# Sliding-window attention and an ELU feed-forward on one core: constants by VectorE arithmetic, the first batch in two halves, x in block order in a ring

## The chip, the cores and the metric

The kernel runs on one core of one Trainium2 chip. The metric is device time in microseconds, the median of several runs, lower is better. A core has five engines that run their own instruction streams and meet at semaphores: TensorE (PE), VectorE (DVE), ScalarE (ACT), GpSimd (POOL) and SyncE (SP), beside 16 DMA engines that the queues of SP and GpSimd feed. PE reads SBUF and writes PSUM, which has eight banks of 128 x 512 float32.

## What is computed

Attention over 8 batches, 8 heads, 576 positions, head size 64, causal with a window of 128 and a slope per head (ALiBi); its output is laid out as 4608 tokens of 512 features and goes through a two-layer feed-forward with ELU.

```python
scores = scale * np.matmul(q, k.transpose(0, 1, 3, 2))
bias = slopes[:, None, None] * (-np.abs(rel))[None, :, :]
mask = (rel >= 0) & (rel < 128)
scores = np.where(mask, scores + bias[None], -1e9)
attn = softmax(scores)
x = np.matmul(attn, v).transpose(0, 2, 1, 3).reshape(B * S, H * D)
h = x @ w_in                                   # 512 -> 2048
g = np.where(h > 0, h, np.exp(np.minimum(h, 0)) - 1)
out = g @ w_out                                # 2048 -> 512, float32
```

## The kernel before

All products are in float16 with float32 sums. Positions 0 to 511 of a batch are four blocks of 128, positions 512 to 575 are its **tail**. Inside a block the 128 positions stand in the order (j, i) for position 4i + j, which comes from the loads: four neighbouring positions lie in one partition row (`stq`, L76), and PE's transposes (L209) take them apart. Queries, keys and the columns of E are all in this **block order**; v is loaded so that its rows agree (L96, four loads of 32 partitions per block of 128).

*Attention* goes by units (a batch and a pair of heads, 32 units). Of a unit:

- `transposes` (L209, 8 on PE) and two copies from PSUM into QK (L215, DVE). QK holds 64 rows of the head and 64 rows of bias: a row of positions, a row of ones, and rows that push block pairs outside the window to a large negative score. These rows are the same for all batches and are filled once.
- `scores` (L245, PE), in two halves of 512 columns for each head (half 0: key blocks 0 and 1, half 1: 2, 3 and the tail), each followed by an exponential on ACT into E (L249).
- `cut` (L253, DVE): the minimum of E (1024 columns) and a table, `band`, that is 60000 inside the window and 0 outside it.
- `values` (L262) and `values_tail` (L273, L274) on PE. VP holds v in 64 columns and ones in the next 64, so the product has the sums of E beside the numerators, in the other 64 partitions.
- `log_den` (L280) and `inv_den` (L284) on ACT: 1/den as exp(-ln den).
- `normalize` (L288, DVE): numerator times 1/den into xT, the transposed x, once per head. Here the block order is undone: the access patterns of all three operands walk (n, j, i), and the output is written to (n, i, j), so that columns of xT are tokens in order. For a batch's tails `normalize_tail` (L306) needs no reordering.

*Feed-forward* goes by blocks of 512 tokens (9) and chunks of 128 of the 2048 (16): 144 steps of `hidden` (L316, four PE products over the 512 features, 512 tokens wide, into a PSUM bank `hp` of which there are two; exponential on ACT, L319; clip on POOL, L320) and `elu` (L325, DVE, reads `hp` and so frees the bank). `output` (L337) multiplies 128 tokens by w_out, 16 products into one bank; ACT copies it to `ob` (L341), and one DMA from SP stores 128 rows (L343).

*The order* is written out by hand, in **slots**. A unit begins every 4 slots (`APS`) and its steps lie at fixed slots behind that. Slot s also has hidden step m = s - LAG, the ELU of step m - 1, and the output products of step m - 16. LAG is 16 + 5 = 21, one batch of attention. In the text of a slot hidden comes first, then ELU, then the attention steps, then output. Each engine executes its own instructions in exactly this order.

*Ahead of slot 0* all constants are built (L118 to L193): the identity, `band` and the window rows by GpSimd's affine_select, then (since TQ and TK must be complete) the bias rows of all 8 heads by DVE (L186) and ACT (L190), and the ones and zeros of VP by DVE (L192, L193). Between them stand in GpSimd's queue the casts of v (L105) and the loads of the weights (L381, L384).

Of the kernel before, what the change touches and what calls it, by code (L numbers as in the profile page):

```python
# [19 lines left out]
def kernel(  # L20
# [15 lines left out]
    NTB = NTOK // 512  # L36
    APS = 4
    ABS = NP * APS
    LAG = ABS + 5
    MID = S // 2  # L40

# [20 lines left out]
    w_in_sb = [const.tile([128, FF], F16, name=f"wi{c}", tag=f"wi{c}") for c in range(4)]  # L62
    w_out_sb = const.tile([128, NFC, DM], F16, name="wo")
    xT = const.tile([128, 4, NTOK], F16, name="xT")


    stq, stt = {}, {}

    def load_qk(b, hs=None):
# [4 lines left out]
        h0, h1 = hs or (0, H)  # L74
        return [
            (lambda w=w, src=src: nc.gpsimd.dma_start(  # L76
                stq[b][:, w, h0:h1, :, :].rearrange("p h j d -> p h (j d)"),
                src[b, h0:h1, 0:512, :].rearrange("h (p j) d -> p h (j d)", j=4)))
            for w, src in ((1, k), (0, q))
        ]  # L80

    def load_tail(b):
        return [
            (lambda w=w, src=src: nc.gpsimd.dma_start(
                stt[b][:, w, :, :], src[b, :, 512:576, :].rearrange("h s d -> s h d")))
            for w, src in ((1, k), (0, q))
        ]

    vf = {}

    def load_v(b, n):

        vf[b, n] = stage.tile([128, H, D], F32, name="vf", tag="vf", bufs=3)
        if n < 4:
            for j in range(4):
                nc.sync.dma_start(  # L96
                    vf[b, n][32 * j:32 * j + 32, :, :],
                    v[b, :, 128 * n + j:128 * n + 128:4, :].rearrange("h p d -> p h d"))
        else:
            nc.sync.dma_start(vf[b, n][0:64, :, :],  # L100
                              v[b, :, 512:576, :].rearrange("h p d -> p h d"))
# [6 lines left out]

    nc.scalar.preload_act_table_set("natural_log_exp_and_others")

    with tc.manual_schedule():
        for hp in range(NP):
            for f in load_qk(0, (2 * hp, 2 * hp + 2)):
                f()
        for f in load_tail(0):
            f()

        make_identity(nc, ident)  # L118

        nc.vector.memset(band, BIG)  # L120

        def keep(cols, pattern, base, cm):
            for h in range(4):
                r = slice(32 * h, 32 * h + 32)
                o = band[r, cols]
                if len(pattern) > 1:
                    o = o.rearrange("p (n j i) -> p n j i", j=4, i=32)
                nc.gpsimd.affine_select(out=o, in_=o, compare_op=ALU.is_ge, fill=0.0,  # L128
                                        base=base(h), pattern=pattern, channel_multiplier=cm)

        W2 = [[128, 2], [1, 4], [4, 32]]
        W1 = [[128, 1], [1, 4], [4, 32]]
        neg = lambda p: [[-x, n] for x, n in p]
# [3 lines left out]
        keep(slice(768, 896), W1, lambda h: -h, -4)  # L137
        keep(slice(896, 960), [[-1, 64]], lambda h: 127 - 128 + h, 4)
        keep(slice(960, 1024), [[1, 64]], lambda h: -32 * h, -1)
# [54 lines left out]
        for n in range(3):  # L194
            load_v(0, n)
        for n in range(5):
            cast_v(0, n)
            if n < 2:
                load_v(0, n + 3)
# [255 lines left out]
```

## Time and profile before

| | us |
|---|---|
| median of 3 runs (433.31 to 434.66) | 434.52 |
| the profiled execution, its own time | 432.81 |
| its span, first to last instruction | 431.1 |
| first scores on PE | 43.72 |
| first hidden product | 79.5 |
| first output product | 127.6 |
| PE / DVE / ACT / POOL busy | 343.0 / 287.7 / 241.8 / 169.8 |

A row of a group reads: line, engine, operation, output<-inputs, shapes, count | busy us, mean ns of one | idle time of the engine ahead of them, and what ended it. A row of the timeline reads: start us, duration us, engine, line, operation. PE's products are pipelined, so the time from one start to the next says more than a product's own duration. PEclk is the share of its full clock that PE was granted.

### The profile page before, as it was taken

What the parts mean: (1) busy time and instruction counts of PE and PEld (TensorE: products, weight loads), DVE (VectorE), ACT (ScalarE), POOL (GpSimd) and SP (SyncE); (2) the same over time, 40 slices, a digit from 0 to 9 for tenths busy, and PEclk for the clock granted to TensorE, in tenths of its full rate; (3) what the DMA queues carried; (4) which work ended last, traced back from release to release, by engine and by line L of the source; (5) the groups of instructions that cost most, each with busy time, mean ns of one, the idle gap of its engine ahead of it and who ended that gap; (6) DMA issues with size and microseconds to landing.
All of it is one profiled execution on the core that took longest, in us unless ns stands there. A gap on an engine that the chain in (4) does not pass through costs nothing.

```text
span 431.1 us, 6246 instructions
## 1 busy us (share of the span) xinstructions
PE 343.0 (80%) x2240; PEld 187.6 (44%) x2240; DVE 287.7 (67%) x396; ACT 241.8 (56%) x445; POOL 169.8 (39%) x289
## 2 busy tenths in 40 slices
PE   0100556766699989998998999899989989999985
PEld 0100434443355545554554555455545544444432
DVE  1018666789878888988898787889888763334400
ACT  1005556566777676676667777766767754434411
POOL 8887323146245423633452355233322223333300
PEclk9999955699999999999999999999999999999999
DMA  9406999929214733661293238230000001101011
GB/s 139 44 1 123 202 191 193 121 53 129 42 24 82 116 82 77 90 120 50 62 133 76 75 61 126 78 90 29 26 24 26 26 24 49 40 36 49 26 56 66
DMA packets 72127, 32.91 MB, mean 76 GB/s; under 512 B 48544, under 2 KB 66976, under 8 KB 72096
## 3 DMA queue, kind: packets, MB, share of 16 engines
q0 software_dynamic: 27872, 13.63, 24.9%
q1 hardware_dynamic: 44224, 18.89, 17.0%
q8 instruction: 17, 0.28, 0.3%
q14 instruction: 14, 0.11, 0.1%
HBM read 36.70 MB, written 9.44 MB: 107 GB/s over the span
## 4 chain that ended last, share of the span: by engine, by line
PE 49%; DVE 30%; POOL 8%; DMA 5%; issue 4%; ACT 3%; POOLq 0%; ACTq 0%; DVEq 0%
PE hp L316 20%; PE op L337 18%; DVE xT L288 13%; DVE g L325 7%; DVE QK L215 7%; DMA stt<-in_q_dram 4%; PE av L262 4%; POOL band L128 3%; PE sp L245 3%; PE tp L209 2%; POOL stq L76 2%; DVE xT L306 1%; DVE E L253 1%; DMA vf<-in_v_dram 1%; ACT e L319 1%
## 5 line engine op out<-in xcount | busy, mean ns | idle before, releaser
L320 POOL TENSOR_SCALAR e<-e 128x512 f32<-128x512 f32 x144 | 90.0, 625 | 216.8 <-ACT e L319 209.1
L316 PE MATMUL hp<-xT,wi 128*128 128x512 f16 x576 | 149.5, 382 | 23.7 <-DVE g L325 23.6
L319 ACT ACTIVATE e<-hp 128x512 f32<-128x512 f32 x144 | 86.0, 597 | 111.6 <-PE hp L316 109.0
L337 PE MATMUL op<-wo,g 128*128 128x512 f16 x576 | 145.9, 379 | 2.9 <-ACT ob L341 2.9
L325 DVE SCALAR_TENSOR_TENSOR g<-e,hp 128x512 f16<-128x512 f32 x144 | 97.1, 687 | 67.9 <-POOL e L320 66.0
L316 PEld LDWEIGHTS <-wi 128*128 128x128 f16 x576 | 56.1, 98 | 93.4 <-issue 32.3
L288 DVE TENSOR_TENSOR xT<-av,rden 64x512 f16<-64x512 f32 x64 | 83.5, 1304 | 2.0
L249 ACT ACTIVATE E<-sp 128x512 f16<-128x512 f32 x128 | 72.5, 595 | 7.1 <-PE sp L245 6.3
L337 PEld LDWEIGHTS <-g 128*128 128x128 f16 x576 | 52.2, 98 | 50.4 <-issue 4.0
L245 PE MATMUL sp<-QK 128*128 128x256 f16 (+2 forms) x384 | 47.4, 249 | 30.6 <-issue 27.4
L245 PEld LDWEIGHTS <-QK 128*128 128x128 f16 x384 | 34.5, 103 | 47.5 <-issue 32.3
L215 DVE COPY QK<-tp 64x1024 f16<-64x1024 f16 x64 | 44.0, 688 | 15.0 <-PE tp L209 14.4
L253 DVE TENSOR_TENSOR E<-E,band 128x1024 f16<-128x1024 f16 x64 | 44.0, 688 | 7.6 <-ACT E L249 7.6
L280 ACT ACTIVATE lden<-av 64x512 f32<-64x512 f32 x64 | 37.5, 587 | 14.7 <-PE av L262 13.9
L262 PE MATMUL av<-E,VP 128*128 128x256 f16 (+1 forms) x256 | 37.6, 272 | 9.2 <-DVE xT L288 8.2
L262 PEld LDWEIGHTS <-VP 128*128 128x128 f16 x256 | 25.5, 102 | 26.1 <-issue 12.0
L341 ACT COPY ob<-op 128x512 f32<-128x512 f32 x36 | 21.5, 597 | 17.9 <-PE op L337 17.9
L105 POOL TENSOR_SCALAR VP<-vf 128x512 f16<-128x512 f32 (+1 forms) x40 | 26.2, 656 | 11.3 <-DMA vf<-in_v_dram 10.5
L209 PE MATMUL tp<-ident,stq 128*128 128x128 f16 x256 | 22.1, 236 | 0.3 <-ACT E L249 0.3
L190 ACT ACTIVATE QK<-TK 64x576 f16<-64x576 f16 (+1 forms) x8 | 3.2, 451 | 32.3 <-DVE QK L180 32.3
L284 ACT ACTIVATE rden<-lden 128x512 f32<-128x512 f32 x32 | 20.2, 630 | 1.0
L176 DVE MEMSET TQ<- 1x576 f16 x1 | 0.5, 538 | 26.3 <-POOL TQ L173 26.3
(44 smaller groups left out, 147.3 us busy)
## 6 DMA issues: line engine op xcount, KB each, us to landing
out_dram<-ob SPq DMA_DIRECT2D x36, 256.0 KB, 2.0
vf<-in_v_dram SPq DMA_DIRECT2D x128, 64.0 KB, 2.4
stq<-in_k_dram POOLq DMA_DIRECT2D x7, 512.0 KB, 6.0
stq<-in_q_dram POOLq DMA_DIRECT2D x7, 512.0 KB, 7.4
wi<-in_moe_w_in_dram POOLq DMA_DIRECT2D x4, 512.0 KB, 9.4
wo<-in_moe_w_out_dram POOLq DMA_DIRECT2D x4, 512.0 KB, 20.1
vf<-in_v_dram SPq DMA_DIRECT2D x8, 128.0 KB, 3.0
stq<-in_k_dram POOLq DMA_DIRECT2D x4, 128.0 KB, 5.9
```

The lines of the kernel that those rows point to most:

```text
L215: nc.vector.tensor_copy(QK[0:64, 2 * hp:2 * hp + 2, :, 0:512].rearrange("p h w (n a i) -> p (h w) n a i", a=2, i=32)[:, :, :, odd, :], t[r ...
L245: nc.tensor.matmul(s[:, o:o + n], kq[:, 1, kc:kc + 128], kq[:, 0, qc:qc + n], start=True, stop=True)
L249: nc.scalar.activation(ex[b, hp, g][:, 512 * half:512 * half + 512], s, AF.Exp, scale=0.125)
L253: nc.vector.tensor_tensor(out=e, in0=e, in1=band, op=ALU.min)
L262: nc.tensor.matmul(a[:, o0:o0 + w], vp[:, n, hp, lo:lo + 128], e[:, e0:e0 + w], start=st, stop=sp)
L280: nc.scalar.activation(lden[b, hp][r, :], avt[b, hp, g][r, :], AF.Ln)
L288: nc.vector.tensor_tensor(out=xT[r, hp, b * S:b * S + 512].rearrange("p (n i j) -> p n j i", j=4, i=32), in0=avt.pop((b, hp, g))[r, :].rea ...
L316: nc.tensor.matmul(p, w_in_sb[c][:, fc * 128:(fc + 1) * 128], xT[:, c, t * 512:(t + 1) * 512], start=(c == 0), stop=(c == 3))
L319: nc.scalar.activation(e, p, AF.Exp)
L320: nc.gpsimd.tensor_scalar(out=e, in0=e, scalar1=1.0, scalar2=0.0, op0=ALU.min, op1=ALU.max)
L325: nc.vector.scalar_tensor_tensor(out=gs[t][:, fc, :], in0=es.pop((t, fc)), scalar=1.0, in1=hps.pop((t, fc)), op0=ALU.subtract, op1=ALU.max)
L337: nc.tensor.matmul(ops[t], gs[t][:, fc, ts * 128:(ts + 1) * 128], w_out_sb[:, fc, :], start=(fc == 0), stop=(fc == NFC - 1))
```

## The change

*Constants.* GpSimd makes four iotas (row number, column number, positions), and VectorE makes everything from them by arithmetic: the identity as column == row, `band` as (distance from the middle)^2 <= 4060, the window rows by a bitwise and of position minus 8 x row. `band`'s first 512 columns come ahead of slot 0, the rest in slot 7. Bias rows are filled head by head in the slots (`bias_rows`: ACT copies the query side, DVE the key side). The ones of VP are now GpSimd's.

*Order at the start.* The first batch's attention runs in two passes: for each pair of heads, every two slots, the first half of the scores, a cut of 512 columns, `values_half` for tokens 0 to 255, `den_half`, `norm_half`; from slot 8 on, every four slots, the same for the second half and the tail. The first half's scores borrow the two `hp` banks. E has 9 buffers, since a pair's E lives until its second half. LAG is 13. Weights are loaded by chunks in the slots (`load_wi` takes 512 columns of all 512 rows), from slot 0 on; v of batch 0 is loaded behind a memset on GpSimd that holds it back behind the loads of q and k.

*Blocks.* The first 512 tokens are two blocks of 256, then 512 as before: 160 hidden steps, of which 32 are of half width, and 189 slots instead of 181.

*x.* xT has 1728 columns (three batches) and is used as a ring; a block that crosses its end is computed in two pieces (8 products instead of 4). Its columns stay in block order, so `normalize` writes one piece of 512. The rows of the output are then in block order too, and each tile is stored by several DMAs of 32 rows, every fourth row of the output, or of 64 rows for a tail.

```diff
-    LAG = ABS + 5
+    RING = 3 * S
...
-    xT = const.tile([128, 4, NTOK], F16, name="xT")
+    xT = const.tile([128, 4, RING], F16, name="xT")
...
-        make_identity(nc, ident)
-        nc.vector.memset(band, BIG)
-        for c0 in (0, 256, 512):
-            keep(slice(c0, c0 + 256), W2, lambda h: -h, -4)
-            keep(slice(c0, c0 + 256), neg(W2), lambda h: 127 + h, 4)
...
+        V.tensor_scalar(out=ident, in0=col, scalar1=rowf, scalar2=None, op0=ALU.is_equal)
...
+        V.tensor_scalar(out=bt[:, 0:256], in0=posi[:, 0:256], scalar1=kmid, scalar2=None,
+                        op0=ALU.subtract)
+        V.tensor_tensor(out=bt[:, 0:256], in0=bt[:, 0:256], in1=bt[:, 0:256], op=ALU.mult)
+        V.tensor_scalar(out=band[:, 0:256], in0=bt[:, 0:256], scalar1=4060.0, scalar2=BIG,
+                        op0=ALU.is_le, op1=ALU.mult)
+        V.tensor_copy(band[:, 256:512], band[:, 0:256])
...
+        def bias_rows(h):
+            c = 8.0 * 2.0 ** (-8.0 * (h + 1) / H)
+            nc.scalar.copy(QK[64:128, h, 0, :], TQ[64:128, :])
+            V.tensor_copy(QK[g_, h, 1, :], TK[g_, :])
+            V.tensor_scalar(out=QK[r_, h, 1, :], in0=TK[r_, :], scalar1=c, scalar2=None, op0=ALU.mult)
...
+        FIRST = ((0, 0, 0, 256), (1, 128, 256, 128))
+        SECOND = ((2, 256, 512, 256), (1, 256, 384, 128), (3, 384, 768, 128))
...
         def normalize(b, hp, g):
-            nc.vector.tensor_tensor(
-                out=xT[r, hp, b * S:b * S + 512].rearrange("p (n i j) -> p n j i", j=4, i=32),
-                in0=avt.pop((b, hp, g))[r, :].rearrange("p (n j i) -> p n j i", j=4, i=32),
-                in1=rden[b, hp][o, :].rearrange("p (n j i) -> p n j i", j=4, i=32), op=ALU.mult)
+            c = xcol(b * S)
+            V.tensor_tensor(out=xT[NUM[g], hp, c:c + 512], in0=avt.pop((b, hp, g))[NUM[g], :],
+                            in1=rden[b, hp][DEN[g], :], op=ALU.mult)
...
+        blocks = [(0, 256), (256, 256)] + [(512 * i, 512) for i in range(1, NTOK // 512)]
...
+            cuts = [(0, n)] if a + n <= RING else [(0, RING - a), (RING - a, n)]
+            for u0, u1 in cuts:
+                x0 = xcol(c0 + u0)
+                for c in range(4):
+                    nc.tensor.matmul(p[:, u0:u1], w_in_sb[:, c, fc * 128:(fc + 1) * 128],
+                                     xT[:, c, x0:x0 + u1 - u0], start=(c == 0), stop=(c == 3))
...
-                nc.sync.dma_start(out[r0:r0 + 128, :], ob)
+                    for p0, rows in rows_of(c0 + 128 * ts):
+                        nc.sync.dma_start(rows, ob[p0:p0 + rows.shape[0], :])
...
+        F = 8
+        base = lambda b: F if b == 0 else F + 16 * b
+        LAG = F + 5
```

How the change stands in the instruction streams, at three places. GpSimd (POOL) behind the first loads of q and k; in the program of before:

```order
L84 DMA stt<-in_q_dram 64x8x64
masks.py:197 MEMSET ident 128x128
masks.py:199 ISA
masks.py:199 AFFINE_SELECT ident<-ident 128x128
L128 AFFINE_SELECT band<-band 32x256 x24
L128 AFFINE_SELECT band<-band 32x128 x4
L128 AFFINE_SELECT band<-band 32x64 x8
L141 IOTA posi 128x512
L143 IOTA posi 128x64
L165 MEMSET TK 32x2x128
```

and in the changed one, where the iotas stand behind the first two of the eight loads:

```order
L72 DMA stq<-in_k_dram 128x2x256
L72 DMA stq<-in_q_dram 128x2x256
L119 ISA
L119 IOTA row 128x1
L120 IOTA col 128x128
L121 IOTA posi 128x512
L123 IOTA posi 128x256
```

The selections and GpSimd's part of TQ and TK (14 more rows in before) are gone. VectorE (DVE) ahead of the first copy of transposed heads (tp into QK); before, the rows of TQ and TK, eight heads' bias rows (only the first are shown), VP:

```order
L176 MEMSET TQ 1x576
L177 TENSOR_SCALAR TQ<-posi 1x576
L176 MEMSET TK 1x576
L177 TENSOR_SCALAR TK<-posi 1x576
L180 MEMSET QK 128x8x128
L186 TENSOR_SCALAR QK<-TK 64x576
L186 TENSOR_SCALAR QK<-TK 64x64
L186 TENSOR_SCALAR QK<-TQ 64x576
```

and now, the end of the arithmetic (gi and gt are the window and position rows on their way to TQ and TK) and the first copies:

```order
L169 TENSOR_SCALAR gi<-posi,gof 32x768
L170 TENSOR_SCALAR gi<-gi 32x768
L171 TENSOR_SCALAR TQ<-gi 32x768
L173 TENSOR_SCALAR TK<-gi 32x768
L175 TENSOR_SCALAR is_159<-rowf 128x1
L176 TENSOR_SCALAR is_160<-rowf 128x1
L177 TENSOR_SCALAR isx<-is_160 128x1
L178 TENSOR_SCALAR gt<-posi 32x768
L179 TENSOR_SCALAR TK<-gt,is_159,is_160 32x768
L181 TENSOR_SCALAR TQ<-gt,isx,is_159 32x768
```

VectorE now waits for GpSimd's iotas alone, and two heads' bias rows follow its copies instead of eight ahead of them. SP's queue, where the first outputs are stored between loads of v:

```order
L100 DMA vf<-in_v_dram 64x8x64
L343 DMA out_dram<-ob 128x512 x2
L96 DMA vf<-in_v_dram 32x8x64 x8
L343 DMA out_dram<-ob 128x512
L96 DMA vf<-in_v_dram 32x8x64 x8
```

```order
L89 DMA vf<-in_v_dram 32x8x64 x8
L405 DMA out_dram<-ob 64x512
L405 DMA out_dram<-ob 32x512 x2
L93 DMA vf<-in_v_dram 64x8x64
L405 DMA out_dram<-ob 32x512 x8
```

Each stored tile is now three or four transfers, in the same places between the loads of v.

More of the change, by code (lines that the diff above doesn't have):

```diff
@@ L111 @@
     with tc.manual_schedule():
[L112 to L116, printed above, removed]
-        make_identity(nc, ident)
-        nc.vector.memset(band, BIG)
[L122 to L129, printed above, removed]
@@ L191 @@
-        for g in range(2):
-            nc.vector.memset(VP[g][:, 4, :, :], 0.0)
-            nc.vector.memset(VP[g][:, :, :, 64:128], 1.0)
[L194 to L199, printed above, removed]
-        spt, tpt, ex, avt, tailt, lden, rden = {}, {}, {}, {}, {}, {}, {}
+        row = const.tile([128, 1], I32, name="row")
+        col = const.tile([128, 128], I32, name="col")
+        posi = const.tile([128, 768], I32, name="posi")
```

440 lines of the change are left out of this document (258 added, 182 removed).

## Prediction

> **What bounds the kernel now.** I read the page first, then busy time by stage, the start of the timeline, one unit of the middle, and the waits of the middle. The stretches below are cut at the first scores (43.7), the first hidden product (79.5), the first output product (127.6), the end of attention (343) and the last hidden product (410.6). Columns: span, then busy us of PE, PEld, DVE, ACT, POOL, the granted clock, DMA share, GB/s.
>
> ```profile
> span 431.1 us, 6246 instructions
> 43.70:79.50 35.80, 21.23 (x167) 15.79 (x168) 25.45 (x32) 20.66 (x37) 9.82 (x14) 0.69 1.28 194
> 79.50:127.60 48.10, 36.28 (x262) 21.05 (x260) 40.41 (x54) 30.86 (x57) 19.35 (x29) 0.95 0.48 68
> 127.60:343.00 215.40, 204.07 (x1429) 113.75 (x1427) 178.12 (x236) 149.58 (x278) 80.41 (x128) 1.00 0.38 72
> 343.00:410.60 67.60, 65.38 (x308) 29.62 (x307) 30.14 (x44) 31.25 (x54) 23.26 (x38) 1.00 0.10 36
> ```
>
> So there are five programs in one. Until 43.7 nothing useful runs. Then 35.8 us of attention alone, in which no engine is over 71% busy. Then 16 slots (21 to 36) of attention and hidden products in 48.1 us, 3.0 us a slot, with DVE the busiest. Then PE at 95%. Then pure products at 1.73 us a slot (67.6 us for 39 slots).
>
> The first 43.7 us, in order of time (start, duration, engine, line):
>
> ```profile
> 1.33 0.89 POOL L76 DMA_DIRECT2D stq<-in_k_dram  x1 [0.81 <-POOLq L439]
> 9.18 15.76 POOL L128 TENSOR_SCALAR_AFFINE_SELECT band<-band 32x256 f16<-32x256 f16 x36
> 15.29 1.03 PE L209 MATMUL tp<-ident,stq 128*128 128x128 f16 x8
> 31.34 0.46 DVE L177 TENSOR_SCALAR TQ<-posi 1x576 f16<-1x576 int32 x1 [1.75 <-POOL TQ L173]
> 38.38 1.12 DVE L193 MEMSET VP<- 128x1280 f16 x1 [0.33 <-DVE VP L192]
> 43.72 1.01 PE L245 MATMUL sp<-QK 128*128 128x256 f16 x6 [27.40 <-issue]
> ```
>
> The heads' data are there at 15.3, since PE transposes them, and the scores wait another 28 us for tables: GpSimd's selections until 31, then VectorE's copies into QK and the memsets of VP.
>
> The middle, one unit of four slots, PE's starts and the normalisations on DVE:
>
> ```profile
> 181.39 0.38 PE L245 MATMUL sp<-QK 128*128 128x256 f16 x2
> 182.00 2.65 DVE L288 TENSOR_TENSOR xT<-av,rden 64x512 f16<-64x512 f32 x2
> 183.36 0.54 PE L262 MATMUL av<-E,VP 128*128 128x256 f16 x4
> 183.74 0.39 PE L245 MATMUL sp<-QK 128*128 128x256 f16 x4
> 183.96 1.03 PE L337 MATMUL op<-wo,g 128*128 128x512 f16 x4
> 185.42 1.02 PE L316 MATMUL hp<-xT,wi 128*128 128x512 f16 x4 [0.43 <-DVE g L325]
> 188.45 0.55 PE L262 MATMUL av<-E,VP 128*128 128x256 f16 x4
> 189.40 1.03 PE L337 MATMUL op<-wo,g 128*128 128x512 f16 x4
> 190.26 1.03 PE L316 MATMUL hp<-xT,wi 128*128 128x512 f16 x4
> 191.12 0.38 PE L245 MATMUL sp<-QK 128*128 128x256 f16 x2
> PE hp L316 <- DVE g L325: 22.0, 25, 2.2
> ```
>
> From one start to the next a group of four 512-wide products takes 0.86 us (189.40 to 190.26), the values 0.38, a half of the scores 0.22, and the values with tails and transposes 0.95. A unit is then 8 x 0.865 + 4 x 0.22 + 0.38 + 0.95 = 9.13 us, 2.28 a slot; it took 9.73 (181.39 to 191.12), and units with a batch's tail more. The batch that starts at 182.00 repeats at 221.81, 39.8 us or 2.49 a slot. The difference is the last row: hidden products wait 22 us (from 80 to 345) for ELU, which stands on VectorE behind two normalisations of 1.3 us each.
>
> ```profile
> 221.81 1.30 DVE xT L288
> L325 DVE SCALAR_TENSOR_TENSOR g<-e,hp 128x512 f16<-128x512 f32 x144 | 97.1, 687 | 67.9 <-POOL e L320 66.0
> L288 DVE TENSOR_TENSOR xT<-av,rden 64x512 f16<-64x512 f32 x64 | 83.5, 1304 | 2.0
> L306 DVE TENSOR_TENSOR xT<-avtail,rdent 64x256 f16<-64x256 f32 x16 | 6.8, 422 | 0.2
> L253 DVE TENSOR_TENSOR E<-E,band 128x1024 f16<-128x1024 f16 x64 | 44.0, 688 | 7.6 <-ACT E L249 7.6
> L215 DVE COPY QK<-tp 64x1024 f16<-64x1024 f16 x64 | 44.0, 688 | 15.0 <-PE tp L209 14.4
> L249 ACT ACTIVATE E<-sp 128x512 f16<-128x512 f32 x128 | 72.5, 595 | 7.1 <-PE sp L245 6.3
> L280 ACT ACTIVATE lden<-av 64x512 f32<-64x512 f32 x64 | 37.5, 587 | 14.7 <-PE av L262 13.9
> L284 ACT ACTIVATE rden<-lden 128x512 f32<-128x512 f32 x32 | 20.2, 630 | 1.0
> L319 ACT ACTIVATE e<-hp 128x512 f32<-128x512 f32 x144 | 86.0, 597 | 111.6 <-PE hp L316 109.0
> ```
>
> (The first row is from the chain of waits, the others are groups: line, engine, tile, shape and count, busy us and mean ns.) VectorE's unit is 4 x 0.687 (ELU) + 2 x 0.688 (cuts) + 2 x 0.688 (copies) + 2 x 1.304 + four tail steps of 0.42 a batch = 8.5 us, 2.13 a slot.
>
> **The change, part by part.** The sum is made in slots of the new program: scores of the first pair at slot 0, first hidden product at slot 13, two half blocks until slot 44, last hidden product at slot 172, last output at 188.
>
> *Constants.* GpSimd's selections go. It issues two loads (0.89 us the first), then four iotas (0.61 the largest before), so VectorE starts at about 3.2. Its chain: 13 of the 26 steps need the one before, at 0.33 us each (L193 behind L192) 4.3; seven 768-wide ones at 0.56 (L177's 0.46 for 576, scaled) 3.9; four 256-wide ones 1.1; the small ones and the memsets 1.9. That is 11.2, done at 14.4. Bounds: 12 if dependent steps cost half of that, 17 if the 768-wide ones run like L325 and L306, where 256 more elements cost 0.265 us (0.95 each). The transposes (15.3 before) are ready by then. Adding the copies of the first transposes (1.4) and two heads' bias rows (four at 0.33), scores start at 17 instead of 43.7.
>
> *First batch in halves.* VectorE's work for a pair of heads: copies 1.38, bias rows 1.3, two half cuts and two half normalisations at 0.42 (L306's 256-wide price; a 512-wide f16 cut has half the elements of the 0.69 one), 4.4. In its order a pair's normalisations stand right behind its cuts, so it waits for values, two logarithms and one exponential of half width: about 0.6 + 2 x 0.35 + 0.4, with hand-overs 2.2. Four pairs at 6.6, tail copies 0.8, the rest of the band 1.5: from 14.4 to 43, and the first cut of the second halves with its values stands ahead of the first hidden product on PE: 44, where before had 79.5. Bounds: 36 if the waits overlap, 53 at the 35.8 us of before. The weight loads run beside it.
>
> *Slots 13 to 44.* Half blocks halve hidden, exponential, clip, ELU. Slots 13 to 28: VectorE 16 x 0.42 for ELU, 4.9 for the second halves of three pairs, 5.9 for tails, copies and cuts of the next batch, and four waits of 1.2 ahead of normalisations: 22.4 us, 1.4 a slot. Slots 29 to 44 add half outputs: per slot ScalarE (4 x 0.595 + 2 x 0.587 + 0.63)/4 + 0.35 + 0.08 = 1.48, about 1.55 with the tails, VectorE 0.42 + (7.3 - 2.75)/4 = 1.56 (7.3 is worked out in the next part), PE 1.43. The middle of before was 0.21 above its busiest engine (2.49 against 2.28), so 1.8: 28.8 us. Slots 45 to 60, full hidden and half output: PE, ScalarE and VectorE all at 1.8 to 1.84, taken as 2.15: 34.4.
>
> ```profile
> out_dram<-ob SPq DMA_DIRECT2D x36, 256.0 KB, 2.0
> vf<-in_v_dram SPq DMA_DIRECT2D x128, 64.0 KB, 2.4
> 188.99 3.88 SPq L96 DMA_DIRECT2D vf<-in_v_dram  x8
> 427.93 0.33 SPq L343 DMA_DIRECT2D out_dram<-ob  x1
> ```
>
> *x in block order.* The normalisation writes and reads in one piece; the nearest rows are L306 (422 ns for 256 elements) and L325 (687 for 512), so 0.69 instead of 1.30. Per unit VectorE falls from 8.5 to 7.3 us, 1.82 a slot, and ELU is early by 1.2 us where PE waits 0.43. PE's 2.28 is next: I take 2.33 for slots 61 to 134, 172.4 us; bounds 2.29 and 2.49. Two of eight blocks wrap around the ring: twice as many, shorter products, 1.5 us in all (0 to 4).
>
> *Stores.* Each 128-row tile leaves in three or four pieces. 0.33 us of issue each on SP, which has room (17 stores of 0.33 and 17 loads of 0.49 a batch, 14 us of 37), and two more ahead of the end: +0.7. A piece costs what v's 64 KB pieces cost, 2.4 us, not four times a whole tile's 2.0. Against this part speaks the Trainium skill, "DMA: Bandwidth & Descriptors", Rules for kernel authors: transfers to separate parts of the partitions run one after the other, so one over all 128 is better. By that rule the last tile would end about 4 us later; the issues of v, eight in 3.88 us, do not agree.
>
> *The sum.* 44 + 22.4 + 28.8 + 34.4 + 172.4 + 1.5 = 303.5. Slots 135 to 172 at 1.73: 65.7. The last outputs and store as before (410.6 to 431.1) 20.5 + 0.7. Span 390.4; the profiled execution took 432.81, 1.7 more than its span: 392.1. The median of the runs, 434.52, is 0.4% above that execution, so 393.7, **394 us**. Its own range, from the bounds, is 380 to 408.
>
> **The rivals.**
>
> *The middle does not gain* (0.12): the normalisation stays at 1.3 us since two float sources and not the order set it, or another wait takes its place. For it: nothing shows a contiguous 512-wide one. Against: L306. 74 x 0.16 more, about 406.
>
> *Latency, not work, sets the half blocks* (0.14): three small steps and four hand-overs a slot keep 2.4 us as full slots have. 16 x 1.0 + 16 x 0.6 = 25.6 more: 419. For it the 3.0 us a slot at 79.5 to 127.6, where no engine was above 84%; against, that late v loads and VectorE explain most of that.
>
> *The clock stays low* (0.09):
>
> ```profile
> 56.00:60.00 4.00, 2.17 (x18) 1.55 (x16) 2.87 (x4) 1.98 (x4) 1.12 (x2) 0.50 1.60 186
> 79.50 1.72 PE hp L316 x4
> 100.00:120.00 20.00, 13.22 (x112) 8.18 (x110) 16.94 (x24) 13.93 (x28) 8.87 (x14) 1.00 0.61 79
> ```
>
> At half clock four products take 1.72 instead of 0.86. If slots 13 to 44 ran so, PE would need 1.85 and 2.85 a slot: 7 and 17 us more, 418. The trace had full clock at 66% busy PE and half at 54%; half blocks on a full clock give about 75%. The Trainium skill, "TensorE: Matmul & The Clock Gate", Why this matters for your kernels, has PE gaps of over about 3 us drop the clock. By that rule my half blocks, whose longest wait is 2.2 us, keep it and 394 stands; if the gaps grow past it, 418.
>
> *SP becomes the bound, slower than before* (0.03): 17 stores and 17 v loads a batch on one queue, where v was loaded in the first stretch at
>
> ```profile
> 58.91 31.23 SPq L96 DMA_DIRECT2D vf<-in_v_dram  x15
> ```
>
> 2.1 us each. If transfers issue so slowly, v comes late, its cast on GpSimd waits, and each clip behind it. Slots 13 to 134 are 7.6 batches and 259 us in my sum; SP sets the pace above 259/(7.6 x 34) = 1.00 us a transfer, and from 1.16 (300 us) the kernel is slower than before. At 1.2 us: 310, so 446. Against: those fifteen waited for buffers, and eight unhindered ones took 3.88.
>
> *Loads in the way at the start* (0.07): the weights, now asked for from about 11 us on, share the engines with q, k and v; first hidden at 54 instead of 44: 404.
>
> **How the numbers follow.** The forecast has 0.55, the rivals the rest. From 380 to 418 all but the slow rival, half of the two near 418 and the forecast's lower end are held, about 0.8. A measurement tells 0.3% from no change. Only the SP rival is not faster: faster 0.96, same 0.01, slower 0.03.
>
> **What would show it.** Scores of the first pair at 17 (13 to 22), first hidden product at 44; the 64x512 normalisation near 690 ns; PE's waits for ELU in the middle under 5 us and batches 37 to 38 us apart; 1.4 and 1.8 us a slot in the half blocks at full clock; SP never waited for. A batch at 39 or more, or a first hidden product after 55, proves a step wrong.

## The result and the profile after

The changed kernel takes 395.56 us (median of 4 runs, 395.1 to 397.05), the kernel before 433.91 beside it (431.45 to 434.66): a ratio of 0.9131, 95% interval 0.9085 to 0.9177. The forecast was 394. The profiled execution took 397.05 us with a span of 395.3.

One number of the kernel before, in the table and in the prediction, is wrong. The first output product is not at 127.6 but at 120.12, as the timeline of before has it (start us, duration us, engine, line, operation):

```profile
118.31 1.03 PE L316 MATMUL hp<-xT,wi 128*128 128x512 f16 x4
...
120.12 1.03 PE L337 MATMUL op<-wo,g 128*128 128x512 f16 x4
```

The hidden products of slots 21 to 36 therefore ran from 79.3 to 118.3, 2.44 us a slot and not 3.0. No term of the sum used the 3.0, but it was the reason given for the rival in which latency sets the half blocks, and that reason was too strong.

Busy time by stage of the kernel after, cut at the first scores, first hidden product, first output, first full blocks of hidden and of output, end of attention, and the point from which output products stand alone (374.0; it answers to 410.6 in before, and the last hidden product is 2.6 us ahead of it in both; columns: span, then busy us of PE, PEld, DVE, ACT, POOL, granted clock, DMA share, GB/s):

```profile
16.39:45.08 28.69, 13.08 (x87) 8.33 (x88) 19.91 (x46) 15.53 (x30) 11.55 (x16) 1.00 1.16 174
45.08:73.70 28.62, 20.47 (x183) 15.95 (x182) 19.01 (x41) 18.54 (x45) 14.27 (x26) 0.88 0.94 142
73.70:100.40 26.70, 23.67 (x217) 16.76 (x214) 23.25 (x42) 21.30 (x47) 12.84 (x24) 1.00 0.61 90
100.40:134.00 33.60, 31.36 (x235) 18.09 (x233) 28.15 (x44) 26.40 (x51) 15.74 (x26) 1.00 0.57 87
134.00:312.00 178.00, 177.52 (x1370) 109.01 (x1368) 133.86 (x206) 131.87 (x244) 68.53 (x110) 1.00 0.41 74
312.00:374.00 62.00, 60.34 (x291) 27.70 (x290) 26.07 (x40) 27.29 (x48) 21.49 (x35) 1.00 0.15 36
374.00:395.30 21.30, 14.44 (x64) 6.12 (x63) 0.45 (x1) 2.34 (x4) 0.00 (x0) 0.97 0.27 63
```

From 134 to 312 PE is busy 177.5 of 178 us, where it had 204 of 215 in the middle of before. The marks in the timeline:

```profile
5.02 0.42 DVE L157 TENSOR_TENSOR bt<-bt 128x256 f32<-128x256 f32 x1
5.48 0.29 DVE L158 TENSOR_SCALAR band<-bt 128x256 f16<-128x256 f32 x1
...
10.42 0.68 DVE L179 TENSOR_SCALAR TK<-gt,is,is 32x768 f16<-32x768 f32 x1
10.71 1.50 POOL L206 MEMSET VP<- 128x1280 f16 x1
11.03 1.60 DVE L181 TENSOR_SCALAR TQ<-gt,isx,is 32x768 f16<-32x768 f32 x1
...
13.58 1.32 DVE L225 COPY QK<-tp 64x1024 f16<-64x1024 f16 x2
...
16.39 1.36 PE L258 MATMUL sp<-QK 128*128 128x256 f16 x4 [10.29 <-DVE QK L191]
...
45.08 1.04 PE L361 MATMUL hp<-xT,wi 128*128 128x256 f16 x4
...
49.63 0.60 PE L361 MATMUL hp<-xT,wi 128*128 128x256 f16 x4
...
64.45 0.61 PE L219 MATMUL tp<-ident,stq 128*128 128x128 f16 x8 [1.76 <-ACT E L262]
...
67.67 1.01 PE L361 MATMUL hp<-xT,wi 128*128 128x256 f16 x4 [1.55 <-DVE g L372]
...
71.38 1.04 PE L361 MATMUL hp<-xT,wi 128*128 128x256 f16 x4
...
100.29 1.03 PE L361 MATMUL hp<-xT,wi 128*128 128x512 f16 x4
...
133.67 1.03 PE L361 MATMUL hp<-xT,wi 128*128 128x512 f16 x4
```

The first rows are steps of the constants. Then come the first copy into QK (13.58, the constants are done), the first scores, and the hidden products of slots 13, 29, 45 and 61; the two rows at 64 and 67 are PE's longest waits in slots 13 to 28.

The column of the granted clock needs care up to 49 us. At 71.38 the views give 0.50, and four products of 256 columns take 1.04 us; at 49.63 they take 0.60. At 45.08 they take 1.04 as well, so PE ran at half its clock there too, though the table has 1.00 for the stage ahead of 45.08: the views print 1.00 for all that lies ahead of the first change of the clock that the trace holds, here the rise at about 49 us. In the kernel before the same holds at the first scores, where six products of scores take 1.01 us (43.72) and later ones 0.60 (127.01).

The groups of the page that answer to L288, L316 and L325 of before:

```profile
L361 PE MATMUL hp<-xT,wi 128*128 128x512 f16 (+5 forms) x768 | 153.4, 330 | 11.5 <-DVE g L372 10.8
L372 DVE SCALAR_TENSOR_TENSOR g<-e,hp 128x512 f16<-128x512 f32 (+1 forms) x160 | 101.0, 634 | 78.0 <-POOL e L365 75.5
...
L331 DVE TENSOR_TENSOR xT<-av,rden 64x512 f16<-64x512 f32 x56 | 38.5, 688 | 1.7
```

The normalisation went from 1304 to 688 ns, and hidden products wait 10.8 us for ELU, VectorE's step that frees their bank, in the whole program, of which 5.1 lie between 80 and 345 (22.0 before):

```profile
PE hp L361 <- DVE g L372: 5.1, 10, 1.0
```

The chain of waits shows one batch after another in the middle, 37.2 us apart where before had 39.8:

```profile
206.05 1.03 PE hp L361 x8
...
243.27 1.02 PE hp L361 x4
```

### The profile page after: what moved, and what is told of

It reads as the page before. It is cut to its first block, busy times and chain, and to the rows that moved or that the text cites. A ratio compares the mean times of both kernels' runs of the same rounds, so it can differ in the third digit from the quotient of the medians.

```text
span 395.3 us, 6838 instructions
## 1 busy us (share of the span) xinstructions
PE 342.1 (87%) x2440; PEld 202.6 (51%) x2440; DVE 262.9 (67%) x448; ACT 246.1 (62%) x465; POOL 158.8 (40%) x261
## 4 chain that ended last, share of the span: by engine, by line
PE 70%; DVE 18%; ACT 4%; issue 3%; POOL 2%; POOLq 0%; ACTq 0%; DVEq 0%
PE hp L361 28%; PE op L399 27%; PE sp L258 6%; PE av L277 5%; DVE QK L225 4%; DVE g L372 3%; PE tp L219 3%; DVE xT L331 2%; DVE xT L345 2%; DVE E L266 1%; DVE QK L190 1%; DVE QK L191 1%; PE avh L288 1%; DVE xT L302 1%; ACT ldent L337 1%
## 5 line engine op out<-in xcount | busy, mean ns | idle before, releaser
L365 POOL TENSOR_SCALAR e<-e 128x512 f32<-128x512 f32 (+1 forms) x160 | 93.5, 585 | 206.6 <-ACT e L364 205.9
L361 PE MATMUL hp<-xT,wi 128*128 128x512 f16 (+5 forms) x768 | 153.4, 330 | 11.5 <-DVE g L372 10.8
L372 DVE SCALAR_TENSOR_TENSOR g<-e,hp 128x512 f16<-128x512 f32 (+1 forms) x160 | 101.0, 634 | 78.0 <-POOL e L365 75.5
L364 ACT ACTIVATE e<-hp 128x512 f32<-128x512 f32 (+1 forms) x160 | 88.8, 555 | 94.3 <-PE hp L361 92.0
L361 PEld LDWEIGHTS <-wi 128*128 128x128 f16 x768 | 73.0, 99 | 79.1 <-issue 17.9
L266 DVE TENSOR_TENSOR E<-E,band 128x1024 f16<-128x1024 f16 (+1 forms) x72 | 45.4, 636 | 1.9 <-ACT E L262 1.6
L331 DVE TENSOR_TENSOR xT<-av,rden 64x512 f16<-64x512 f32 x56 | 38.5, 688 | 1.7
L277 PE MATMUL av<-E,VP 128*128 128x256 f16 x224 | 31.4, 264 | 0.5
L219 PEld LDWEIGHTS <-stq 128*128 128x128 f16 x256 | 16.6, 104 | 7.4 <-DMA stq<-in_k_dram 4.6
L189 ACT COPY QK<-TQ 64x768 f16<-64x768 f16 x8 | 6.2, 825 | 10.7 <-DVE TQ L181 10.6
## 6 DMA issues: line engine op xcount, KB each, us to landing
wo<-in_moe_w_out_dram POOLq DMA_DIRECT2D x4, 512.0 KB, 21.2
```

The costliest lines, as they stand in the source:

```text
L219: nc.tensor.transpose(t[:, g, w, :, j, :], stq[b][:, w, 2 * hp + g, 2 * j:2 * j + 2, :].rearrange("p a d -> p (a d)"), ident)
L266: V.tensor_tensor(out=e, in0=e, in1=band[:, c0:c1], op=ALU.min)
L277: nc.tensor.matmul(a[:, o:o + w], VP[b % 2][:, n, hp, lo:lo + 128], ex[b, hp, g][:, e:e + w], start=(i == 0), stop=(i == 3))
L331: V.tensor_tensor(out=xT[NUM[g], hp, c:c + 512], in0=avt.pop((b, hp, g))[NUM[g], :], in1=rden[b, hp][DEN[g], :], op=ALU.mult)
L361: nc.tensor.matmul(p[:, u0:u1], w_in_sb[:, c, fc * 128:(fc + 1) * 128], xT[:, c, x0:x0 + u1 - u0], start=(c == 0), stop=(c == 3))
L364: nc.scalar.activation(e[:, 0:n], p[:, 0:n], AF.Exp)
```

## The experiments

Ratios are to the kernel before, on the same chip, with 95% intervals. In the "parts" below the kernel before is changed in one respect, in the others the kernel after.

**The parts: constants alone.** The change's constants, all ahead of slot 0; the rest as before.

```diff
-        make_identity(nc, ident)
-        nc.vector.memset(band, BIG)
...
+        V.tensor_scalar(out=ident, in0=col, scalar1=rowf, scalar2=None, op0=ALU.is_equal)
...
+            nc.scalar.copy(QK[64:128, h, 0, :], TQ[64:128, :])
+            V.tensor_copy(QK[g_, h, 1, :], TK[g_, :])
```

> The kernel before with the constants of the change alone (all bias rows and the whole band still ahead of slot 0, no halves, normalisation and stores as before). My theory: the gain at the start carries through whole. VectorE ends its 26 steps at 13.6, then 16 bias rows at 0.36 and the rest of the band 1.5, so first scores at about 22 instead of 43.7 and the time about 21 us less, 412. Rival (loads in the way): the weights and the next batch's q and k fill the DMA engines as long as before, the first hidden product comes less than 12 us earlier than 79.5, and the time is above 420.

It took 417.16 us, 0.9638 (0.9596 to 0.968): 16 us less. Scores start at 26.8 and not at 22, the first hidden product at 63.4. So the step that failed is the length of the start; what it gained, 16.9 us at the first scores, came through whole. The middle is as before, as its waits between 80 and 345 show:

```profile
PE hp L333 <- DVE g L342: 20.8, 23, 2.2
```

**The parts: block order alone.**

```diff
-                out=xT[r, hp, b * S:b * S + 512].rearrange("p (n i j) -> p n j i", j=4, i=32),
-                in0=avt.pop((b, hp, g))[r, :].rearrange("p (n j i) -> p n j i", j=4, i=32),
...
+                out=xT[r, hp, b * S:b * S + 512],
+                in0=avt.pop((b, hp, g))[r, :],
...
-                nc.sync.dma_start(out[r0:r0 + 128, :], ob)
+                for p0, rows in rows_of(r0):
+                    nc.sync.dma_start(rows, ob[p0:p0 + rows.shape[0], :])
```

> The kernel before with x left in block order and the rows put right by the stores, nothing else. My theory: VectorE's normalisations are what PE waits for behind ELU; they fall to 0.69, the middle from 2.49 to 2.33 us a slot over 90 slots (14 us), the stage without output from 3.0 to about 2.7 (5 us), the first batch by about 4: 411 in all. Rival (the middle does not gain by it, the wait goes to another engine): batches stay at 39 us or more and the time is above 425.

411.96 us, 0.9511 (0.9477 to 0.9545): 21 us less, as expected. The first hidden product stays at 78.5, the first output comes at 113.6, so this stage took 35.1 us instead of 40.8, and the rest was gained in the middle, where PE is busy 177.4 of 178 us and waits less for ELU (two views of this kernel, the stretch 134 to 312 and the waits from 80 to 345):

```profile
134.00:312.00 178.00, 177.40 (x1257) 100.50 (x1256) 136.49 (x211) 132.28 (x245) 69.36 (x111) 1.00 0.44 80
```

```profile
PE hp L316 <- DVE g L325: 8.6, 8, 1.4
```

**The parts: both of these together**, without halves, half blocks or bias rows in slots.

> Both of the above together: the change without its two halves of the first batch, half blocks and late weight loads. My theory, if the parts add: 434 - 21 - 22 = about 391, as good as the whole change, so that the halves are worth nothing. Rival (the halves carry a third of the gain, as their earlier first hidden product, 45 against about 58 here, suggests): 400 to 408.

396.32 us, 0.9145 (0.9113 to 0.9178). The two parts add up (16 + 21 of 37), and together they are as fast as the whole change (395.56). What it has beyond them (halves, half blocks, bias rows in slots, another order of loads, the ring) brings nothing in sum that this measurement can tell. So the theory's claim held, though 391 was too low; the rival fell. Busy time of this kernel from its first hidden product to its first output, from there to 134, and from the start to 134; then of the kernel after from the start to 134:

```profile
63.30:97.90 34.60, 26.79 (x223) 16.43 (x221) 28.40 (x46) 26.34 (x51) 16.58 (x25) 0.99 0.60 85
97.90:134.00 36.10, 35.98 (x252) 20.09 (x250) 28.17 (x45) 26.72 (x51) 16.16 (x25) 1.00 0.49 81
0.00:134.00 134.00, 86.24 (x650) 53.81 (x651) 99.85 (x172) 80.93 (x145) 65.33 (x98) 0.90 0.79 121
```

```profile
0.00:134.00 134.00, 89.79 (x720) 59.81 (x721) 102.55 (x203) 84.61 (x172) 68.83 (x117) 0.97 0.83 121
```

The kernel after starts its hidden products 18 us earlier (45.1 against 63.3), but at 134 both stand at the same work: 64 output products and 162 of scores are done in each, and 32.5 hidden steps, counted in 512 tokens, against 33. (Busy time alone does not tell this: four products of 256 columns are busy for 1.04 us at half clock and for 0.60 at full.) PE then has 252.3 us of busy time left in the kernel after (342.1 in all, less 89.8) and 251.7 in this one (337.9 less 86.2), is full in both from there on, and they end together.

The 18 us were lost ahead of 134. From its first hidden product to 134 PE is idle for 13.4 us in the kernel after (its three stages from 45.08 to 134) and for 7.9 in this one. The other 12.7 are busy time, of the second halves of the first batch's attention, which the kernel after still has to do behind its first hidden product, of half clock, and of more and shorter products; how they divide was not measured.

**Load on VectorE.** In the kernel after each full normalisation is made a second time, into a scratch tile that nobody reads.

```diff
+            for o in (xT[NUM[g], hp, c:c + 512], twice[NUM[g], :]):
+                V.tensor_tensor(out=o, in0=a[NUM[g], :], in1=rden[b, hp][DEN[g], :], op=ALU.mult)
```

> The changed kernel with each full normalisation made twice, the second time into a scratch tile: VectorE's load per unit is again that of before (8.7 us against 8.5) with contiguous patterns. My theory (load on VectorE ahead of ELU sets the middle): batches go back from 37.2 to about 39.5 us, PE again waits for ELU, time about 15 us more, 410. Rival (it was the order of columns itself, by PE's reads of xT or PSUM's banks, not VectorE's time): under 4 us more.

417.93 us, 0.9655 (0.962 to 0.9691): 22 us more than the kernel after, where 15 were expected. Two normalisations of 0.69 cost VectorE what one of 1.30 did, a batch lasts what it lasted before, 39.8 us, and between 134 and 312 PE again waits 11.0 us for ELU (9.1 in before, none in the kernel after):

```profile
L334 DVE TENSOR_TENSOR xT<-av,rden 64x512 f16<-64x512 f32 x56 | 38.6, 689 | 1.7
...
L334 DVE TENSOR_TENSOR twice<-av,rden 64x512 f16<-64x512 f32 x56 | 38.1, 680 | 0.0
```

```profile
180.25 1.02 PE hp L363 x4
...
220.03 1.03 PE hp L363 x8
```

So it is VectorE's time ahead of ELU that sets the middle, and neither the order of x nor the stores as such. That it came to more than 15 has its place ahead of the middle: the hidden product of slot 61 is already 7.3 us late (140.98 against 133.67), so VectorE's load counts in slots 29 to 60 too. With this load the time is that of the constants alone (417.16).

**Half blocks away, first pass kept in halves.**

```diff
-        blocks = [(0, 256), (256, 256)] + [(512 * i, 512) for i in range(1, NTOK // 512)]
+        blocks = [(512 * i, 512) for i in range(NTOK // 512)]
...
-        LAG = F + 5
+        LAG = F + 16 + 3
```

> The changed kernel with nine blocks of 512 tokens instead of two half ones and eight: hidden products begin at slot 27 (the first batch keeps its two passes), 187 slots. Theory from the three runs before (half blocks are worth nothing: full blocks begin two slots earlier, and the slots that lose their half products get shorter, about 1.1 us): slot 27 at 60, then 16 slots at 2.05, 92 at 2.33, 36 at 1.73 and 21: 391 to 396. Rival (half blocks use PE's idle time, about 8 us of products, and keep its clock up): 402 or more.

399.68 us, 0.9238 (0.9195 to 0.9282), between theory and rival. The first hidden product is at 62.6, no earlier than in the kernel without halves, though scores start at 16.4 and not 26.6. The way from scores to hidden is 46.2 us against 36.7 there, so attention in two passes, with the bias rows in its slots, gives back the 10 us that the earlier scores brought, and half blocks are worth some 4 us in that arrangement.

**First batch in whole units, full blocks, quick start.** The order of before, with the change's bias rows in slots, and with the loads of the second batch's q and k ahead of those of the weights. The tail steps of the first batch also come two slots later than in the kernel after.

```diff
-        F = 8
-        base = lambda b: F if b == 0 else F + 16 * b
-        LAG = F + 5
+        base = lambda b: 16 * b
+        LAG = 16 + 5
...
+            at(1, load_qk, 1, w)
...
+            at(1, load_wi, i)
```

> The changed kernel's start (constants, bias rows pair by pair) with whole units for the first batch as in the kernel before, full blocks from slot 21 on, and the loads in another order: the next batch's q and k ahead of the weights. Theory (what the whole change gave at the start is the constants and bias rows; of the first batch's 36 us about 17 are waits for q and k of the next batch): scores at 17, units at about 7.5 us, first hidden product at 50 to 52, 16 slots at 2.1, then the middle: 381 to 386. Rival (two passes are what shortens the first batch): first hidden product after 60, 393 or more.

391.52 us, 0.9056 (0.9019 to 0.9092), better than the change by about 1%: the intervals just overlap, the times of the runs do not (391.23 to 392.74 against 395.1 to 397.05). The first hidden product is at 58.0 and not at 50 to 52, so the theory's 381 to 386 failed, and so did the rival's product after 60. Between 18 and 70 PE waits 10.7 us in its two banks `av` for normalisations:

```profile
PE av L272 <- DVE xT L326: 10.7, 4, 3.9
```

**The same with the second head's second scores ahead of the first head's values** in the first batch, so that PE has work in that wait.

```diff
+                if b == 0:
+                    at(s + 3, scores, b, hp, 1, 1)
...
-                at(s + 3, scores, b, hp, 1, 1)
+                if b > 0:
+                    at(s + 3, scores, b, hp, 1, 1)
```

> The last but one (whole units for the first batch, full blocks from slot 21) with one step moved in the first batch: the second scores of a unit's second head ahead of the first head's values in PE's order. Theory (a unit of 8.4 us there is one loop: normalisation frees the PSUM bank, values, then scores, exponential, cut, values, denominators, normalisation of the second head, since PE stands at the first head's values): the second head's scores, exponential and cut leave the loop, units at 6.5 to 7, first hidden product at 51 to 53 instead of 58, time 385 to 387. Rival (VectorE's copies and bias rows or the loads set the 8.4): first hidden product at 57 or later, 390 or more.

389.65 us, 0.9004 (0.8984 to 0.9025), the fastest kernel of this study, and its interval lies below that of the change. The wait fell to 6.4 us and the first hidden product came 3.2 us earlier, at 54.8, but the first output at 92.2 and the last hidden product at 366.0 are where they were (92.4, 366.2). So the expected 385 to 387 failed: the 3 us were lost again before 92. The trace shows where. The first hidden step is 3.2 us ahead of the one without the move, the second 2.35 (57.71 against 60.06): the clock is at 0.50 from 54 to 56, and this first step runs in it. The seventh is still 2.35 ahead (67.98 against 70.33), the eighth 0.5 (71.99 against 72.49), since PE has to wait there for the tails of the second batch's q, which are still in transfer; without the move the same transposes start at 71.90 and wait for nothing:

```profile
71.65 0.40 PE L232 MATMUL tpt<-ident,stt 64*128 64x64 f16 x8 [2.04 <-DMA stt<-in_q_dram]
```

So behind the loop that the theory saw, the loads of the second batch are the next bound, as the rival has it.

**Order of loads.** The kernel with both parts, its second batch's q and k loaded ahead of the weights.

```diff
-        for f in pre:
-            f()
...
+        for f in pre:
+            f()
```

> The kernel before with the change's constants and contiguous normalisation (396.3), with q and k of the second batch loaded ahead of w_in instead of behind it. Theory (5.2 us of PE's wait for the tail of the second batch's q is the load order): first hidden product at about 58 instead of 63.3, time 391 to 392. Rival (the wait only goes on to the next load, v or the weights, or to the loop through PSUM): 394 or more.

393.22 us, 0.9092 (0.9067 to 0.9118): the first hidden product moves from 63.3 to 58.9, and 3 us of the 4.4 reach the end. The kernel of the two parts so comes within 2 us of whole units with a quick start, which had this order of loads too; so this order, and the later tail steps (last experiment), may be most of what that one gained over the change; neither was tried alone in it.

**The half normalisation later on VectorE.**

```diff
+            if hp > 0:
+                at(s + 1, norm_half, hp - 1, 0)
...
-            at(s + 3, norm_half, hp, 0)
+            if hp == NP - 1:
+                at(s + 3, norm_half, hp, 0)
```

> The changed kernel with the half normalisations of pairs 0 to 2 put behind the next copies and bias rows in VectorE's order. My theory (VectorE waits 1.8 us for the half denominators in each of the first two pairs, 0.15 in the third): first hidden product at 41.5 instead of 45.1 and 3.5 us less, 392. Rival (PE's or ScalarE's chain ends last, the wait only moves): within 1 us of 395.6.

396.18 us, 0.9151 (0.9119 to 0.9183), first hidden product at 44.4: nothing. VectorE no longer waits for ScalarE there, it now waits for PE's transposes, which stand in PE's order behind the same chain:

```profile
23.90 1.39 DVE L225 COPY QK<-tp 64x1024 f16<-64x1024 f16 x2 [1.42 <-PE tp L219]
```

**Stores whole.** Each tile leaves in one store of 128 rows, 36 stores instead of 136; the rows of the output then stand in block order.

```diff
-                    for p0, rows in rows_of(c0 + 128 * ts):
-                        nc.sync.dma_start(rows, ob[p0:p0 + rows.shape[0], :])
+                    r0 = c0 + 128 * ts
+                    nc.sync.dma_start(out[r0:r0 + 128, :], ob)
```

> The changed kernel with each tile stored whole, 128 rows by one transfer (the rows of the output then stand in block order). My theory: stores by pieces cost SP's issues at the end alone, 0.7 us, so 394.9. By the rule that transfers to separate parts of the partitions run one after the other: about 4 us less at the end, 391.5. If SP's queue held back v's loads anywhere: more than that.

**Stores in halves of a piece**, 272 stores.

```diff
-                        nc.sync.dma_start(rows, ob[p0:p0 + rows.shape[0], :])
+                        n = rows.shape[0] // 2
+                        for o in (0, n):
+                            nc.sync.dma_start(rows[o:o + n, :], ob[p0 + o:p0 + o + n, :])
```

> The changed kernel with every store cut in two again, 16 rows (32 for a tail): 272 stores, 34 stores and 17 loads of v a batch on SP. My theory (SP has room below about 1.0 us a transfer, or 37 us a batch): 34 x 0.33 + 17 x 0.49 = 20 us a batch, no change in the middle, about 1 us more at the end: 396.5. Rival of the prediction (SP sets the pace, v comes late and the clips on GpSimd wait): 410 or more, with GpSimd waiting for v in the middle.

395.49 us, 0.9133 (0.91 to 0.9166) with 36 stores, and 396.63, 0.9167 (0.9143 to 0.9192) with 272: over the whole range of seven to one the time moves by 1.1 us, within the intervals, which overlap. The piece stores of the kernel after land in less than the 2.0 us of a whole tile before (KB each, us from issue to landing):

```profile
out_dram<-ob SPq DMA_DIRECT2D x128, 64.0 KB, 1.7
```

Behind the last products a price does show. From the start of the last sixteen output products to the end of the span it is 7.45 us with whole stores (386.35 to 393.8; 7.48 in before), 8.32 with pieces (386.98 to 395.3) and 9.18 with halves of them (385.32 to 394.5), so about 0.9 us for each cut, near the 0.7 that the prediction and the theory of the whole stores put down. In the medians it hardly stands out.

The Trainium skill, "DMA: Bandwidth & Descriptors", Rules for kernel authors, has it that two transfers to separate halves of the partitions run one after the other, so that one over all 128 is to be taken. By that rule the whole stores should have ended about 4 us earlier, an estimate of the prediction from that page; the traces show 0.9 us, and the measurement decides. In the middle, beside products, pieces cost nothing that these runs show. The rival with SP as the bound falls as well.

**The first batch's tails two slots later.** In the kernel after ScalarE does three tail steps at 62.7 us, and VectorE two, in slot 24.

```diff
-                e = s + 6 if b else s + 4
+                e = s + 6
```

> This is the kernel after with the first batch's tail denominators and tail normalisation moved from slot 24 to slot 26; nothing else differs. In the kernel after, ScalarE makes three tail steps (0.77 us each pair) ahead of the exponentials at 62.7 us, TensorE waits 1.76 us for these and 1.55 us for VectorE's g at 66, and its granted clock is 0.5 from 68 to 72. Theory: these steps are what stands in the way, so with them two slots later both waits shrink, the clock stays at 1.0 until 74, slots 13 to 28 take some 24 us instead of 26.3, and the whole takes 393 (392 to 394.5). Rival: the same work on ScalarE and VectorE is in the way two slots later just as well; the wait and the low clock only move, the first output stays at 73 to 74 or the first 128x512 hidden product at 100, and the whole stays within 1 us of the kernel after.

393.62 us, 0.909 (0.9063 to 0.9117). The intervals of this kernel and the kernel after overlap, the times of their runs do not (392.84 to 395.02 against 395.1 to 397.05). The profiled execution of the kernel after was its slowest, so the kernels with whole and with halved stores, whose steps are the same up to the first output, stand beside it here. Slots 13 to 28 took 24.6 us, in the other three 26.3, 25.8 and 25.2. The first output comes at 70.73, there at 73.71, 73.0 and 72.0; the batch that starts at 206.05 in the kernel after starts at 203.12, in the other two at 205.43 and 204.41. So it is 1.3 to 2.9 us earlier. Stretches of 2 us (columns as above, the seventh number is the granted clock), first of the kernel after, then of this one:

```profile
62.00:64.00 2.00, 0.69 (x9) 0.48 (x7) 0.90 (x4) 1.93 (x6) 0.40 (x1) 1.00 1.45 212
64.00:66.00 2.00, 1.30 (x14) 1.07 (x14) 1.96 (x5) 1.22 (x4) 0.76 (x1) 1.00 1.45 182
66.00:68.00 2.00, 0.45 (x4) 0.26 (x2) 1.89 (x4) 0.81 (x2) 0.52 (x2) 0.63 0.69 91
68.00:70.00 2.00, 2.00 (x14) 1.52 (x12) 0.38 (x1) 0.91 (x2) 0.40 (x1) 0.50 0.00 0
70.00:72.00 2.00, 2.00 (x13) 1.45 (x12) 1.04 (x3) 1.87 (x5) 0.45 (x1) 0.50 0.00 0
```

```profile
62.00:64.00 2.00, 1.48 (x17) 1.15 (x15) 1.94 (x5) 1.50 (x4) 0.82 (x2) 1.00 1.40 193
64.00:66.00 2.00, 0.41 (x5) 0.22 (x4) 1.91 (x4) 1.92 (x5) 0.61 (x2) 1.00 1.45 179
66.00:68.00 2.00, 2.00 (x15) 1.50 (x13) 1.44 (x4) 1.10 (x3) 0.40 (x1) 0.50 0.65 84
68.00:70.00 2.00, 2.00 (x15) 1.60 (x14) 1.08 (x2) 1.89 (x4) 0.45 (x1) 0.65 0.00 0
70.00:72.00 2.00, 2.00 (x25) 1.60 (x23) 1.77 (x4) 1.79 (x5) 0.63 (x1) 1.00 0.00 0
```

One of two waits went (of 1.76 us for the exponentials, now 0.52), the other stayed (1.58, for ELU), and the clock still falls. It is at half for 3.4 us here and for 6.8 in the kernel after, as the clocks of the stretches add up; but 3.4 it is in the kernel with halved stores as well, with both waits in place:

```profile
66.00:68.00 2.00, 0.92 (x7) 0.73 (x7) 1.32 (x3) 0.45 (x2) 0.20 (x1) 0.87 0.50 64
68.00:70.00 2.00, 2.00 (x14) 1.47 (x13) 0.67 (x2) 1.54 (x4) 0.40 (x1) 0.50 0.00 0
70.00:72.00 2.00, 2.00 (x25) 1.74 (x24) 1.54 (x3) 1.96 (x5) 0.70 (x2) 0.77 0.00 0
```

So this one profile does not show that the later steps shorten the low clock. The mean clocks of all runs speak for it: three of the six of this kernel have 0.997 to 1.0, too high for 3.4 us at half clock behind the first rise, and are its fastest (392.84 to 393.3); the twelve of the other three kernels have 0.989 to 0.994. The theory's time and its tail steps hold; that the clock stays up seems to hold in half of the runs.

## Why the prediction was right, step by step

- *Constants*: done at 13.58 (forecast 14.4), scores at 16.39 (17). Two terms inside were off and made up for each other. Steps that need the one before start some 0.04 us behind its end (5.48 behind 5.02 + 0.42), where 0.33 had been put down for each hand-over. The seven 768-wide steps took 6.05 us and not 3.9; the longest, 1.60, ran beside a GpSimd memset of 1.50.
- *First batch in halves*: 28.7 us from scores to hidden (forecast 27), so 45.08 for 44. That the chain of latencies and VectorE's order set this pace agrees with the later normalisation, which only moved the wait.
- *Slots 13 to 28*: the term that was mis-sized, 26.3 us instead of 22.4, 1.64 a slot and not 1.4. This is 3.9 of the 4.9 us by which the span (395.3) missed 390.4; the kernels with other stores, the same in these slots, took 25.8 and 25.2. The forecast had four waits of 1.2 us and a full clock; the trace has half clock until some 49 us, tail steps ahead of exponentials, waits of 1.76 and 1.55 us, and half clock again for 6.8 us behind them. Moving the tail steps brought the stage to 24.6. What each of these costs by itself was not measured.
- *Slots 29 to 44 and 45 to 60*: 28.9 and 33.4 us (28.8 and 34.4).
- *From slot 61 to the last hidden product*: 240.3 us to 374.0 (239.6). The normalisation is at 688 ns (0.69), batches 37.2 apart (37 to 38), the wait for ELU is 5.1, a trace above the "under 5" of the forecast. The doubled normalisation shows the cause, since it brings the 39.8 of before back. The 1.5 us put down for the two blocks that wrap around the ring came to some 0.3: in the chain of waits their eight products take 0.87 us (203.60) where four take 0.86 (208.39), in 32 steps.
- *End*: 21.3 us (21.2). The 0.7 put down for stores by pieces is there: whole stores save 0.9.
- *Median against profile*: the 0.4% added for it had the wrong sign, since this profiled execution was the slowest of four. That it brought the forecast 1.6 us nearer to the median was luck; the span itself was 4.9 too low.

Of the rivals, the contiguous normalisation not gaining, SP and the loads fell by these numbers. The low clock came, but for some 11 us of the 32 slots (4 until 49 us, 6.8 later), though the second time no wait was longer than 1.76 us and the prediction took its 2.2 for safe. Latency and this clock are what the trace shows behind the 3.9 us of the half blocks.

What the forecast did not ask is what each part is worth by itself. It got the marks of the start right, but its sum counts the halves' early hidden product as the way to the end. The runs show that the same end is reached without halves: a hidden product that begins earlier brings the end forward only if PE has less left to do when it becomes the bound.

## What to carry to other kernels

Where one engine is full from some point to the end, judge a change ahead of that point by the work this engine still has there and not by the first product's time: pieces that start earlier, but leave other work of this engine for later and leave it idle between them, can give all of it back. In a stage where an in-order engine gates the bound, look for strided access patterns in what stands ahead of the gating step; here that was the whole gain of the middle. After a change of several parts, time each part alone, since one of them may carry none of it.

## What was not expected of the hardware

- The same 64 x 512 product of two float operands took 1304 ns with (n, j, i) patterns on all three operands and 688 ns in one piece. By the kernel's text the two inputs are read in order of address in both; only the output was written with a step of four elements. Whether that step or the longer pattern costs the time no run here separates.
- TensorE's granted clock fell to 0.5 behind waits of 1.76 and 1.55 us, some 1.4 us of work between them (62.7 to 67.7 us). The Trainium skill, "TensorE: Matmul & The Clock Gate", Why this matters for your kernels, names idle gaps of over about 3 us for that. Here the clock fell behind two shorter ones close together, and in the last experiment behind one of 1.58 us that followed a stretch of 2 us in which PE was 74% busy; by their mean clocks, three of that kernel's six runs had no such fall.
- Stores of 16, 32 or 128 rows, 272 to 36 of them, took the same time in the whole kernel within 1.1 us; behind the last product each cut in pieces costs some 0.9 us.
